# One core, agent attention and a mixture of experts: buffers of the experts' matrices, pacing of the token loads and the order of SyncE's queue

## The chip, the core and the metric

The kernel runs on one core of a Trainium2 chip. The core has five engines with queues of their own: TensorE (PE; PEld is its weight load), VectorE (DVE), ScalarE (ACT), GpSimd (POOL) and SyncE (SP), which computes nothing and issues most of the transfers. Sixteen DMA engines carry the transfers. The metric is the device time of one execution in microseconds (us), the median of the runs.

## What is computed

Four batches of 11456 tokens with 128 channels, 49 agents, 8 experts. Attention through agents gives one row for each token, and that row goes through one expert, a two-layer network whose hidden width is 1024:

```python
s = scale * agents @ k.T ; a2k = softmax(s over tokens) ; agent_v = a2k @ v
q2a = softmax(scale * q @ agents.T over agents) ; x = q2a @ agent_v
logits = normalise(x) @ normalise(expert_emb).T / tau
e = argmax(logits) ; gate = softmax(logits)[e]
out = gate * (relu(x @ w1[e]) @ w2[e])
```

Inputs and outputs are float32.

## The kernel before

**Units, tiles, steps.** The tokens of a batch are cut into 11 units of 128 x 8 tokens and one of 96 x 2. A unit of K, V or Q is one load of 512 KB (`unit_load`, L103 to L116) into the pool `ld`, 11 buffers that K, V, Q and also the two weight matrices of an expert (`load_expert`, L560 to L566) share. The expert layers run over tiles of 512 tokens, two to a unit: 23 tiles a batch, 8 hidden blocks f each, so 184 steps a batch and 736 in all. Step i is `ffn_mm1(i)` (L740, L741: two 512-column matmuls of high and low parts into hp; then hh on ACT, L744, and hl on DVE, L745) and `ffn_mm2(i - 4)` (L762 to L764: twelve 128-column matmuls into yp).

**One expert for a batch.** The kernel picks the likeliest expert of a batch (`pick_expert`, L487), reads its number on SP (`value_load`, L561: a TENSOR_LOAD), loads its w1 (w1s) and w2 (w2s), folds w1 with the batch's agent values into gh and gl (L520, L537, L538), splits w2 into w2h (ACT) and w2l (POOL, L550 and L551), and then the steps of that batch use gh, gl, w2h and w2l alone. Tokens of another expert ("strays") are marked and done one by one (`stray`).

**Work beside the steps.** While the steps of one batch run, generators do the rest, each advanced by a clock `now` of half steps; `yield n` puts a generator off by n steps. A K or Q unit: `split` squares and scales it on ACT (L313, L317), scales and subtracts it on POOL (L318, L319), and has SP transpose the result by DMA (L321, kT or qT); 8 steps later `scores` (L332 to L334, 24 small matmuls) stand behind the layers' last matmul on PE. A Q unit goes on to exponents (e) and a second transposing DMA (tt, L607), and after 8 more steps to its routing matmuls (rtp, L617 and L618); tt is what the layers' first matmul reads. A V unit: POOL subtracts (kd), ACT takes the exponent, PE multiplies (avp, L422).

**What sets the order.** The builder's scheduler orders every engine's instructions by a timeline of its own. Up to the first step SP is held to the order in which the code is traced (`manual_schedule`, L1082). From then on SP's order is the scheduler's as well, so loads and transposing DMAs stand on SP where its timeline puts them; `keys` (L1026) traces a load up to three units ahead of the K or V unit that is due, and `queries` (L1064) one Q unit ahead, all in one go. The due times of K and V are the table W_ (L1030), in parts of a batch's 184 steps.

Of the kernel before, what the change touches and what calls it, by code (L numbers as in the profile page):

```python
# [19 lines left out]
P = 128  # L20
# [10 lines left out]
def kernel(ctx: ExitStack, tc: tile.TileContext, q, k, v, agents, emb, tau, w1, w2, out):  # L31
# [24 lines left out]
    XB = 5  # L56

# [8 lines left out]
    ld = ctx.enter_context(tc.tile_pool(name="ld", bufs=11))  # L66
# [15 lines left out]

    def big(name, w=D):
        return ld.tile([P, UJ * W], F32, name=name, tag="ld")[:, : UJ * w].rearrange("p (c d) -> p c d", d=w)
# [4 lines left out]
    units = {}  # L89
# [13 lines left out]
    def unit_load(x, kind, b, u):  # L103
        if (kind, b, u) in units or b >= B or u >= NU:
            return
        p, n = ushape(u)
        one = kind == "v"
        s = big(kind + "t", W if one else D)
        if one:
            pool.memset(s[:, :, D:], 1.0)  # L110
        if u < NU - 1:
            src = x[b, : P * J, :].rearrange("(p j) d -> p j d", j=J)[:, u * UJ : u * UJ + n, :]
        else:
            src = x[b, P * J :, :].rearrange("(p j) d -> p j d", j=REM_J)
        sp.dma_start(out=s[:p, :n, :D], in_=src)
        units[kind, b, u] = s  # L116

# [183 lines left out]
    def split(kind, b, u, g):  # L301

        s = units[kind, b, u]
        p, n = ushape(u)

        while ffn_at[0] and len(xs_at) >= XB and not (xs_at[-XB] and now[0] >= xs_at[-XB] + 2 * XT):
            yield 1
        i = len(xs_at)
        xs_at.append(0)
        sq = sm.tile([P, 1], F32, name="usq", tag=kind + "usq", bufs=3)[:p]  # L310
        xs = wk.tile([P, UJ, 2, D], F16, name=kind + "s", tag="xs", bufs=XB)
        with in_place(h_last):
            act.activation(xs[:p, :n, 0], s[:p, :n], AF.Square, accum_out=sq)  # L313
        yield g
        hs = half_scale(sq, 14, kind + "u", 4, *([qbias] if kind == "q" else []))
        sc, iv = yield from hs
        act.activation(xs[:p, :n, 0], s[:p, :n], AF.Copy, scale=sc)  # L317
        pool.tensor_tensor(out=s[:p, :n], in0=s[:p, :n], in1=sc.unsqueeze(2).broadcast_to([p, n, D]), op=ALU.mult)  # L318
        pool.tensor_tensor(out=xs[:p, :n, 1], in0=s[:p, :n], in1=xs[:p, :n, 0], op=ALU.subtract)  # L319
        xT = wk.tile([P, 2 * UJ, P], F16, name=kind + "T", tag="xT", bufs=XB)  # L320
        sp.dma_start_transpose(out=xT[:, : 2 * n, :p], in_=xs[:p, :n].rearrange("p c h d -> p (c h d)"))  # L321
        xs_at[i] = now[0]
        return xT, iv
# [62 lines left out]
    def k1_f32(b, u):  # L386
# [5 lines left out]
        kT = pe_T(units["k", b, u], p, n)  # L392
        yield 2
# [10 lines left out]
    def k2_unit(b, u, eng, g):  # L404
# [15 lines left out]
        for c in range(n):  # L420
            hs = slice(LO * (c % 2), LO * (c % 2) + LO)
            pe.matmul(out=avp[hs, :W], lhsT=de[:p, c * A : c * A + LO], rhs=src[:p, c, :], start=(c < 2), stop=(c >= n - 2),  # L422
                      skip_group_check=True)
        if kb.k2 == 0:
# [135 lines left out]
    def load_expert(ei):  # L560
        ev = sp.value_load(ei[:1, :1], min_val=0, max_val=E - 1)  # L561
        w1s = big("w1s").rearrange("p a b -> p (a b)")
        w2s = big("w2s")
# [7 lines left out]
    def q_unit(b, u, g):  # L571
# [5 lines left out]
        if f32:  # L577
            xT = pe_T(units["q", b, u], p, n)
            yield 1
# [26 lines left out]
        else:  # L606
            sp.dma_start_transpose(out=tt[:, : n * p].rearrange("k (c p) -> k c p", p=p),  # L607
# [195 lines left out]
    def stray():  # L803
# [112 lines left out]
        yield 2  # L916
        h = big("sh")
        NH = 4
# [9 lines left out]
        for f in range(NF):  # L928
            pe.matmul(out=t_[:, :D], lhsT=h[:, f, :], rhs=w2s[:, f, :], start=(f == 0), stop=(f == NF - 1))
            if f % 2 == 1:  # L930
                yield 1
        o = sm.tile([P, D], F32, name="so", tag="so", bufs=1)
# [93 lines left out]
    def keys():  # L1026

        S = NT * NF

        W_ = [(0, 0.25, 0.3, 0.8), (-0.5, 0.25, 0.3, 0.8), (-0.5, 0.25, 0.3, 0.8)]  # L1030
        ops = []
        for b in range(1, B):
            k0, k1_, v0, v1 = (S * (b - 1 + x) for x in W_[b - 1])
            us = range(NEXT if b == 1 else 0, NU)
            ops += [(k0 + (k1_ - k0) * i / len(us), "k", b, u) for i, u in enumerate(us)]
            ops += [(v0 + (v1 - v0) * u / NU, "v", b, u) for u in range(NU)]
        ops.sort()
        start = now[0] // 2
        for i, (at, kind, b, u) in enumerate(ops):
            while now[0] // 2 < start + at:  # L1040
                yield 1
            for _, kd, lb, lu in ops[: i + 3]:
                unit_load(k if kd == "k" else v, kd, lb, lu)
# [20 lines left out]
    def queries():  # L1064
        for b in range(B):
            for u in range(NU):
                if b == 0 and u < LEAD:
                    continue
                for i in (b * NU + u, b * NU + u + 1):
                    unit_load(q, "q", i // NU, i % NU)  # L1070
                spawn(q_unit(b, u, (1, 8, 1, 1, 8, 2)), 2)
                yield UT * NF if u < NU - 1 else NF
# [14 lines left out]
    ffn_at[0] = now[0]  # L1087
    if B > 1:
# [3 lines left out]
    for i in range(nsteps):  # L1092
        b, t, f = ffn_steps[i]
        while not (hasattr(batches[b], "iall") and (b, unit_of(t)[0]) in tts):
            run_step()
        run_half()
        with tc.high_priority(200):
            ffn_mm1(i)
        if i >= LAG:
            step2(i - LAG)  # L1100
        run_half()
# [43 lines left out]
```

## Time and profile before

| | |
|---|---|
| time, median of 3 runs | 1070.23 us (1069.75 to 1071.07) |
| profiled execution, own time | 1072.67 us |
| its span (first to last instruction) | 1070.9 us |
| mean granted TensorE clock | 0.97 of 2.4 GHz |
| PE, PEld, DVE, ACT, POOL busy | 94%, 75%, 72%, 67%, 55% |
| moved by DMA | 152.63 MB, mean 143 GB/s |

The first step begins about 103 us into the span. The page gives shares of busy time over the whole span; the stretches differ, so the tables by stretch and the waits of single lines are read beside it. Matmuls are pipelined: a busy PE has work in flight, and the gaps before its instructions tell what it waited for.

### The profile page before, as it was taken

The page shows a single profiled execution, that of the slowest core. Times are in us where ns is not written, and L with a number is a line of the kernel's source. Part 1 is how long each engine was busy: PE and PEld are TensorE (multiplying, and loading weights), DVE is VectorE, ACT ScalarE, POOL GpSimd, SP SyncE. Part 2 cuts the span into 40 slices and gives each one's busy share as a digit, 9 for nine tenths or more (in the row PEclk, how much of TensorE's full clock was granted, in tenths as well). Part 3 has the DMA queues.
Part 4 walks back from the last instruction along what each step waited for, and adds up shares of the span by engine and source line. Part 5 has one row for each costly group of instructions (what it writes and reads, how often), then busy time and mean ns, then how long its engine had stood idle before and what let it go on. Part 6 is the DMA issues. An engine that isn't in the chain of part 4 may idle for free.

```text
span 1070.9 us, 33823 instructions
## 1 busy us (share of the span) xinstructions
PE 1008.5 (94%) x13878; PEld 806.6 (75%) x13878; DVE 769.5 (72%) x1779; ACT 722.6 (67%) x1406; POOL 583.8 (55%) x653
## 2 busy tenths in 40 slices
PE   7876989999997989999999898999999999999997
PEld 7764767777776877777777776777777777877776
DVE  5664777676687676676787776766678798677785
ACT  3445987676778776666777875766666666666553
POOL 2333995676667763746757774645444544543300
PEclk9776999999999999999999999999999999999999
DMA  9548999568649794557658997355136244442101
GB/s 337 162 103 224 233 227 243 120 148 193 113 113 269 158 202 121 120 138 179 150 95 231 215 190 143 83 129 133 45 72 176 59 127 91 104 80 61 47 31 36
DMA packets 283944, 152.63 MB, mean 143 GB/s; under 512 B 208315, under 2 KB 260619, under 8 KB 283787
## 3 DMA queue, kind: packets, MB, share of 16 engines
q1 hardware_dynamic: 270603, 126.98, 53.9%
q10 hardware_dynamic: 13120, 23.47, 6.4%
q8 instruction: 109, 1.79, 0.7%
q14 instruction: 48, 0.39, 0.1%
q0 software_dynamic: 64, 0.00, 0.0%
HBM read 75.80 MB, written 23.53 MB: 93 GB/s over the span
## 4 chain that ended last, share of the span: by engine, by line
PE 71%; DMA 10%; DVE 5%; POOL 5%; ACT 4%; issue 3%; SPq 0%; ACTq 0%; POOLq 0%; DVEq 0%
PE yp L762 12%; PE hp L740 12%; PE yp L764 11%; PE yp L763 11%; PE hp L741 11%; DMA kT<-ks 5%; PE avp L422 5%; DMA qT<-qs 2%; PE sp L396 2%; ACT hh L744 1%; PE sp L332 1%; DMA tt<-e 1%; PE fTp L378 1%; PE sp L333 1%; PE sp L334 1%
## 5 line engine op out<-in xcount | busy, mean ns | idle before, releaser
L745 DVE SCALAR_TENSOR_TENSOR hl<-hp,hh 128x512 f16<-128x512 f32 (+1 forms) x736 | 480.0, 670 | 167.5 <-ACT hh L744 147.7
L744 ACT ACTIVATE hh<-hp 128x512 f16<-128x512 f32 (+1 forms) x736 | 419.0, 591 | 225.1 <-PE yp L764 89.6
L762 PE MATMUL yp<-w2h,hh 128*128 128x128 f16 (+1 forms) x2880 | 519.2, 220 | 0.0
L763 PE MATMUL yp<-w2l,hh 128*128 128x128 f16 (+1 forms) x2880 | 518.8, 219 | 0.3 <-DVE w2l L548 0.3
L764 PE MATMUL yp<-w2h,hl 128*128 128x128 f16 (+1 forms) x2880 | 518.7, 219 | 0.0
L762 PEld LDWEIGHTS <-hh 128*128 128x128 f16 (+1 forms) x2880 | 284.6, 99 | 45.7 <-issue 6.1
L763 PEld LDWEIGHTS <-hh 128*128 128x128 f16 (+1 forms) x2880 | 284.3, 99 | 42.2 <-issue 0.6
L764 PEld LDWEIGHTS <-hl 128*128 128x128 f16 (+1 forms) x2880 | 284.0, 99 | 39.3 <-issue 0.5
L740 PE MATMUL hp<-tt,gh 128*128 128x512 f16 (+1 forms) x736 | 276.6, 376 | 3.0 <-DVE hl L745 3.0
L741 PE MATMUL hp<-tt,gl 128*128 128x512 f16 (+1 forms) x736 | 276.5, 376 | 0.0
L318 POOL TENSOR_TENSOR qt<-qt,hsc 128x1024 f32<-128x1024 f32 (+1 forms) x46 | 82.1, 1785 | 88.2 <-ACT qs L317 75.8
L319 POOL TENSOR_TENSOR qs<-qt,qs 128x1024 f16<-128x1024 f32 (+1 forms) x46 | 92.2, 2004 | 2.3
L599 POOL TENSOR_TENSOR e<-qe,e 128x392 f16<-128x392 f32 (+1 forms) x46 | 39.7, 862 | 98.2 <-ACT e L598 89.4
L740 PEld LDWEIGHTS <-gh 128*128 128x128 f16 x736 | 72.2, 98 | 7.5 <-issue 6.6
L741 PEld LDWEIGHTS <-gl 128*128 128x128 f16 x736 | 72.2, 98 | 5.9 <-issue 5.2
L318 POOL TENSOR_TENSOR kt<-kt,hsc 128x1024 f32<-128x1024 f32 (+1 forms) x36 | 64.3, 1786 | 22.3 <-ACT ks L317 22.0
L777 DVE TENSOR_TENSOR ot<-yp,gs 128x512 f32<-128x512 f32 (+1 forms) x92 | 61.8, 671 | 17.0 <-PE yp L764 16.3
L319 POOL TENSOR_TENSOR ks<-kt,ks 128x1024 f16<-128x1024 f32 (+1 forms) x36 | 72.7, 2021 | 0.9
L665 POOL TENSOR_TENSOR nrm<-quad,half 128x16 f32<-128x16 f32 (+2 forms) x28 | 68.2, 2435 | 2.0
L422 PE MATMUL avp<-vt,kd 128*64 128x129 f32 x720 | 60.6, 295 | 6.8 <-issue 3.9
L422 PEld LDWEIGHTS avp<-vt,kd 128*64 128x64 f32 x720 | 44.2, 144 | 23.2 <-issue 17.3
L634 POOL TENSOR_TENSOR rt<-rt,qe 128x392 f32<-128x392 f32 (+1 forms) x48 | 47.1, 981 | 26.5 <-ACT rt L633 25.6
(264 smaller groups left out, 1449.5 us busy)
## 6 DMA issues: line engine op xcount, KB each, us to landing
kt<-in_k_dram SPq DMA_DIRECT2D x44, 512.0 KB, 6.2
qt<-in_q_dram SPq DMA_DIRECT2D x44, 512.0 KB, 5.9
vt<-in_v_dram SPq DMA_DIRECT2D x44, 512.0 KB, 4.9
out_dram<-ot ACTq DMA_DIRECT2D x88, 256.0 KB, 2.1
w1s<-in_moe_w_dram SPq DMA_DIRECT2D x5, 512.0 KB, 3.7
w2s<-in_moe_w_dram SPq DMA_DIRECT2D x5, 512.0 KB, 5.3
qT<-qs SPq DMA_TRANSPOSE x46, 5.0
tt<-e SPq DMA_TRANSPOSE x46, 3.2
```

The costliest lines, as they stand in the source:

```text
L318: pool.tensor_tensor(out=s[:p, :n], in0=s[:p, :n], in1=sc.unsqueeze(2).broadcast_to([p, n, D]), op=ALU.mult)
L319: pool.tensor_tensor(out=xs[:p, :n, 1], in0=s[:p, :n], in1=xs[:p, :n, 0], op=ALU.subtract)
L422: pe.matmul(out=avp[hs, :W], lhsT=de[:p, c * A : c * A + LO], rhs=src[:p, c, :], start=(c < 2), stop=(c >= n - 2), skip_group_check=True)
L665: pool.tensor_tensor(out=nrm, in0=quad[:, :n], in1=half[:, :n], op=ALU.pow)
L740: pe.matmul(out=hp[:, :m], lhsT=bt.gh[:, fs], rhs=tt, start=True, stop=False)
L741: pe.matmul(out=hp[:, :m], lhsT=bt.gl[:, fs], rhs=tt, start=False, stop=True)
L744: h_last[:] = [act.activation(hh[:, :m], hp[:, :m], AF.Relu)]
L745: dve.scalar_tensor_tensor(out=hl[:, :m], in0=hp[:, :m], scalar=0.0, in1=hh[:, :m], op0=ALU.max, op1=ALU.subtract)
L762: pe.matmul(out=y, lhsT=hh[:, cs], rhs=bt.w2h[:, f, :], start=(f == 0 and c == 0), stop=False, skip_group_check=True)
L763: pe.matmul(out=y, lhsT=hh[:, cs], rhs=bt.w2l[:, f, :], start=False, stop=False, skip_group_check=True)
L764: y_last[:] = [pe.matmul(out=y, lhsT=hl[:, cs], rhs=bt.w2h[:, f, :], start=False, stop=last, skip_group_check=True)]
L777: dve.tensor_tensor(out=o[:p, :n], in0=yp[:p, :n], in1=gate, op=ALU.mult)
```

## The change

- w1s and w2s get a buffer each of their own (`bufs=1`); the pool `ld` shrinks from 11 buffers to 9 (LB).
- `used` and `room` keep a list of who took each `ld` buffer in turn and at which step its last reader was traced; a load in the layers is traced only when the buffer nine back was last read three steps ago or more.
- `plan` lists K, V and Q units with their due steps; a new generator, `loader`, traces at most one load a step, 18 steps ahead of the due step. `keys` and `queries` no longer load.
- In `split`, 5 steps lie between POOL's subtraction and the transposing DMA; before the DMA of tt, 4 steps. The 8 steps after each DMA stay.
- W_ of batch 1: K over 0 to 0.4 of a batch (was 0 to 0.25), V over 0.43 to 0.83 (was 0.3 to 0.8). Batches 2 and 3 keep theirs.
- The loop over the steps is traced under `manual_schedule` for SP: SP's order is that of the code there. The other engines stay the scheduler's.

```diff
-    ld = ctx.enter_context(tc.tile_pool(name="ld", bufs=11))
+    ld = ctx.enter_context(tc.tile_pool(name="ld", bufs=LB))          # LB = 9
+    ring = []
     def big(name, w=D):
+        ring.append([name, None])
+    def used(*unit):
+        ring[slot[unit]][1] = now[0]
+    def room():
+        at = ring[-LB][1] if len(ring) >= LB else -99
+        return at is not None and now[0] >= at + 2 * 3
 ...
         pool.tensor_tensor(out=xs[:p, :n, 1], in0=s[:p, :n], in1=xs[:p, :n, 0], op=ALU.subtract)
+        used(kind, b, u)
+        if ffn_at[0]:
+            yield 5
         xT = wk.tile([P, 2 * UJ, P], F16, name=kind + "T", tag="xT", bufs=XB)
         sp.dma_start_transpose(out=xT[:, : 2 * n, :p], in_=xs[:p, :n].rearrange("p c h d -> p (c h d)"))
 ...
-        w1s = big("w1s").rearrange("p a b -> p (a b)")
-        w2s = big("w2s")
+        w1s = ld.tile([P, F], F32, name="w1s", tag="w1s", bufs=1)
+        w2s = ld.tile([P, NF, D], F32, name="w2s", tag="w2s", bufs=1)
 ...
         else:
+            if ffn_at[0]:
+                yield 4
             sp.dma_start_transpose(out=tt[:, : n * p].rearrange("k (c p) -> k c p", p=p),
 ...
-        W_ = [(0, 0.25, 0.3, 0.8), (-0.5, 0.25, 0.3, 0.8), (-0.5, 0.25, 0.3, 0.8)]
+        W_ = [(0, 0.4, 0.43, 0.83), (-0.5, 0.25, 0.3, 0.8), (-0.5, 0.25, 0.3, 0.8)]
+    AHEAD2 = 18
+    def loader():
+        kv, qs = plan()
+        start = now[0] // 2
+        X = {"k": k, "v": v, "q": q}
+        for at, kind, b, u in sorted(kv + qs):
+            if (kind, b, u) in units:
+                continue
+            while now[0] // 2 < start + at - AHEAD2 or not room():
+                yield 1
+            unit_load(X[kind], kind, b, u)
+            yield 1
 ...
-            for _, kd, lb, lu in ops[: i + 3]:
-                unit_load(k if kd == "k" else v, kd, lb, lu)
 ...
-                for i in (b * NU + u, b * NU + u + 1):
-                    unit_load(q, "q", i // NU, i % NU)
-                spawn(q_unit(b, u, (1, 8, 1, 1, 8, 2)), 2)
-                yield UT * NF if u < NU - 1 else NF
+            while now[0] // 2 < start + at + 2:
+                yield 1
+            spawn(q_unit(b, u, (1, 8, 1, 1, 8, 2)))
 ...
-    for i in range(nsteps):
+    spawn(loader())
+    with tc.manual_schedule(engines={mybir.EngineType.SP}):
+        for i in range(nsteps):
 ...
```

What the two built programs then hold, at three places. The names are the tiles with their numbers; DMA lines are loads, DMA_TRANSPOSE lines the transposing DMAs.

SP, near the end of batch 0's steps, behind the second batch's expert read and weight loads. Before:

```order
L321 DMA_TRANSPOSE kT_5846<-ks_5732 128x16x128
L607 DMA_TRANSPOSE tt_5778<-e16_1_152 128x8x128
L321 DMA_TRANSPOSE qT_5977<-qs_5870 128x16x128
L115 DMA kt_6091<-in_k_dram 128x1024
L115 DMA qt_6314<-in_q_dram 128x1024
L115 DMA kt_6450<-in_k_dram 128x1024
L115 DMA kt_6739<-in_k_dram 128x1024
L115 DMA qt_6741<-in_q_dram 128x1024
L115 DMA kt_7057<-in_k_dram 96x256
L115 DMA qt_7186<-in_q_dram 128x1024
L321 DMA_TRANSPOSE kT_6197<-ks_6125 128x16x128
```

The same place on SP now:

```order
L338 DMA_TRANSPOSE kT_5939<-ks_5599 128x16x128
L629 DMA_TRANSPOSE tt_5851<-e16_1_152 128x8x128
L338 DMA_TRANSPOSE qT_6057<-qs_5766 128x16x128
L128 DMA kt_6176<-in_k_dram 128x1024
L128 DMA qt_6228<-in_q_dram 128x1024
L338 DMA_TRANSPOSE kT_6296<-ks_6032 128x16x128
L629 DMA_TRANSPOSE tt_6398<-e16_0_151 128x8x128
L128 DMA kt_6562<-in_k_dram 128x1024
L338 DMA_TRANSPOSE qT_6564<-qs_6350 128x16x128
L338 DMA_TRANSPOSE kT_6621<-ks_6428 128x16x128
```

Seven loads stood in a row ahead of a transposing DMA; now there are two, then one, between transposing DMAs.

SP, just before the first step, around the first batch's expert read. Before:

```order
L321 DMA_TRANSPOSE qT_748<-qs_721 128x16x128
L607 DMA_TRANSPOSE tt_816<-e16_0_151 128x8x128
L321 DMA_TRANSPOSE kT_836<-ks_804 128x16x128
L321 DMA_TRANSPOSE kT_1109<-ks_855 128x16x128
L561 TENSOR_LOAD e0i_877
```

The same place on SP now:

```order
L338 DMA_TRANSPOSE qT_748<-qs_721 128x16x128
L128 DMA kt_1062<-in_k_dram 128x1024
L128 DMA qt_1105<-in_q_dram 128x1024
L128 DMA kt_1121<-in_k_dram 128x1024
L128 DMA kt_1166<-in_k_dram 128x1024
L128 DMA qt_1195<-in_q_dram 128x1024
L629 DMA_TRANSPOSE tt_816<-e16_0_151 128x8x128
L338 DMA_TRANSPOSE kT_836<-ks_804 128x16x128
L580 TENSOR_LOAD e0i_877
```

Five loads of the layers' stage came ahead of the expert read, and one transposing DMA went behind it.

POOL, where the second batch's w2 is split (w2s, then w2l). Before:

```order
L318 TENSOR_TENSOR kt_5372<-kt_5372,hsc_6148 128x1024
L669 TENSOR_TENSOR nrm_5879<-ls_5882,nrm_5879 128x8
L550 TENSOR_TENSOR w2s_5610<-w2s_5610,hsc_6049 128x1024
L453 MEMSET avT_16054 128x128
L319 TENSOR_TENSOR ks_6125<-kt_5372,ks_6125 128x8x128
L676 TENSOR_TENSOR lga_5872<-lga_5872,cc_5919 128x64
L551 TENSOR_TENSOR w2l_5833<-w2s_5610,w2h_5832 128x1024
```

The same place on POOL now:

```order
L332 TENSOR_TENSOR qt_5592<-qt_5592,hsc_6373 128x1024
L698 TENSOR_TENSOR lga_6017<-lga_6017,cc_6066 128x64
L333 TENSOR_TENSOR qs_6350<-qt_5592,qs_6350 128x8x128
L707 TENSOR_SCALAR el_6120<-esa_6018 128x8
L708 TENSOR_TENSOR el_6120<-el_6120,l_6026 128x8
L569 TENSOR_TENSOR w2s_5825<-w2s_5825,hsc_6206 128x1024
L472 MEMSET avT_16025 128x128
L332 TENSOR_TENSOR kt_5787<-kt_5787,hsc_6449 128x1024
L570 TENSOR_TENSOR w2l_5987<-w2s_5825,w2h_5986 128x1024
```

A Q unit's two large operations moved ahead of the split of w2 and a K unit's subtraction behind it.

Two counts along the whole orders, of hh on ACT and of hp on PE. From a unit's scaled copy on ACT (L317) to its first score matmul on PE (L332) there lie, over the units in the layers, 10 to 19 steps before (mean 15 for K, 13 for Q) and 15 to 31 now (mean 19 for K, 20 for Q). And the second batch's gp matmuls (L520), which need its w1s, stand at step 165 before and at step 177 now; that batch's steps begin at 184.

## Rows read from the trace of the kernel before

**Rows 1.** The page: PE over the span, and its slices.
```profile
PE 1008.5 (94%) x13878; PEld 806.6 (75%) x13878; DVE 769.5 (72%) x1779; ACT 722.6 (67%) x1406; POOL 583.8 (55%) x653
...
L740 PE MATMUL hp<-tt,gh 128*128 128x512 f16 (+1 forms) x736 | 276.6, 376 | 3.0 <-DVE hl L745 3.0
```

**Rows 2.** Stretches of 25 us: busy of each engine, granted clock, DMA share, GB/s.
```profile
core 0: us, PE busy (x) PEld busy (x) DVE busy (x) ACT busy (x) POOL busy (x), PEclk, DMA share, GB/s
...
125.00:150.00 25.00, 23.06 (x365) 18.20 (x362) 18.25 (x47) 22.54 (x44) 24.67 (x23) 1.00 1.10 187
150.00:175.00 25.00, 22.87 (x372) 18.61 (x373) 17.52 (x40) 20.67 (x38) 21.81 (x19) 1.00 1.16 254
...
325.00:350.00 25.00, 19.34 (x280) 15.09 (x279) 17.03 (x42) 18.87 (x37) 20.20 (x22) 0.90 1.09 266
...
425.00:450.00 25.00, 25.00 (x342) 19.52 (x341) 18.96 (x37) 18.59 (x36) 18.38 (x20) 1.00 0.47 117
...
1025.00:1050.00 25.00, 25.00 (x315) 19.42 (x313) 18.58 (x44) 13.68 (x23) 0.09 (x1) 1.00 0.09 33
```

**Rows 3.** PE's waits, whole span: for what, us in total, times, longest us.
```profile
engine line waited for: us in total, times, longest us
PE sp L332 <- DMA kT<-ks: 18.2, 8, 5.7
...
PE rtp L617 <- DMA tt<-e: 3.7, 3, 1.8
...
PE sp L332 <- DMA qT<-qs: 3.0, 4, 1.8
PE hp L740 <- DVE hl L745: 3.0, 3, 2.2
```

**Rows 4.** The longest such wait: ACT's copy, then the chain of work.
```profile
327.26 1.16 ACT L317 ACTIVATE ks<-kt,hsc 128x1024 f16<-128x1024 f32 x1
...
332.89 2.09 POOL ks L319
335.01 12.93 DMA kT<-ks
347.94 0.05 issue
347.99 0.22 PE sp L332
```

**Rows 5.** SP's DMAs of L321: how long SP stood, ns, and landing.
```profile
L321 SPq DMA_TRANSPOSE qT<-qs x46: 1180/2364/7407, 61.3 to 992.3; - x46
L321 SPq DMA_TRANSPOSE kT<-ks x36: 1181/2938/7696, 84.6 to 662.7; - x36
...
DMA to landing us min/median/max: 2.3/5.1/12.9
```

**Rows 6.** Short stretches from the three longest waits on, columns as in Rows 2.
```profile
342.00:348.00 6.00, 0.34 (x3) 0.02 (x2) 2.14 (x5) 3.00 (x5) 5.79 (x4) 0.76 1.14 184
348.00:352.00 4.00, 4.00 (x52) 3.98 (x53) 0.98 (x2) 0.92 (x2) 0.57 (x2) 0.51 1.20 281
...
403.00:406.00 3.00, 3.00 (x32) 1.87 (x31) 0.75 (x2) 2.41 (x5) 1.49 (x2) 0.52 0.01 3
...
652.00:655.00 3.00, 3.00 (x33) 1.81 (x31) 0.75 (x2) 2.42 (x5) 1.43 (x2) 0.55 0.03 6
```

**Rows 7.** Start-up: ACT's wait for a K unit, PE's first step.
```profile
70.67 1.06 ACT L313 ACTIVATE ks<-kt 128x1024 f16<-128x1024 f32 x1 [2.89 <-DMA kt<-in_k_dram]
...
102.77 0.61 PE L740 MATMUL hp<-tt,gh 128*128 128x512 f16 x1
```

**Rows 8.** The chain that ended last, in order of time: start us, us, what.
```profile
91.72 6.88 DMA w2s<-in_moe_w_dram
98.62 1.15 ACT w2h L541 x2
```

**Rows 9.** The split of the second batch's w2 on POOL.
```profile
335.19 2.15 POOL L551 TENSOR_TENSOR w2l<-w2s,w2h 128x1024 f16<-128x1024 f32 x1
```

**Rows 10.** SP's own waits from 104 us on: total us, times, longest us.
```profile
SPq L115 <- PE avp L422: 96.1, 17, 10.7
```

More of the change, by code (lines that the diff above doesn't have):

```diff
@@ L56 @@
     XB = 5
+    LB = 9
     groups = [[0]]
@@ L88 @@
     now = [0]
-    units = {}
+    units, slot = {}, {}
+    def used(*unit):
[3 more added lines that the diff above has]
+        return at is not None and now[0] >= at + 2 * 3
     def tshape(t):
@@ L116, in unit_load @@
         units[kind, b, u] = s
+        slot[kind, b, u] = len(ring) - 1
     a_sb = sm.tile([A, B, C], F32, name="a_sb", tag="a_sb", bufs=1)
@@ L392, in k1_f32 @@
         kT = pe_T(units["k", b, u], p, n)
+        used("k", b, u)
         yield 2
@@ L423, in k2_unit @@
                       skip_group_check=True)
+        used("v", b, u)
         if kb.k2 == 0:
@@ L578, in q_unit @@
             xT = pe_T(units["q", b, u], p, n)
+            used("q", b, u)
             yield 1
@@ L916, in stray @@
         yield 2
+        while not room():
+            yield 1
         h = big("sh")
+        hs = len(ring) - 1
         NH = 4
@@ L931, in stray @@
                 yield 1
+        ring[hs][1] = now[0]
         o = sm.tile([P, D], F32, name="so", tag="so", bufs=1)
@@ L1024, in first, with plan @@
             now_run(batches[0].pick)
-    def keys():
-        S = NT * NF
-        W_ = [(0, 0.25, 0.3, 0.8), (-0.5, 0.25, 0.3, 0.8), (-0.5, 0.25, 0.3, 0.8)]
-        ops = []
+    S = NT * NF
+    def plan():
+        W_ = [(0, 0.4, 0.43, 0.83), (-0.5, 0.25, 0.3, 0.8), (-0.5, 0.25, 0.3, 0.8)]
+        kv, qs, at = [], [], 0
         for b in range(1, B):
@@ L1034, in keys @@
             us = range(NEXT if b == 1 else 0, NU)
-            ops += [(k0 + (k1_ - k0) * i / len(us), "k", b, u) for i, u in enumerate(us)]
-            ops += [(v0 + (v1 - v0) * u / NU, "v", b, u) for u in range(NU)]
-        ops.sort()
-        start = now[0] // 2
-        for i, (at, kind, b, u) in enumerate(ops):
+            kv += [(k0 + (k1_ - k0) * i / len(us), "k", b, u) for i, u in enumerate(us)]
+            kv += [(v0 + (v1 - v0) * u / NU, "v", b, u) for u in range(NU)]
+        for b in range(B):
+            for u in range(NU):
+                if b > 0 or u >= LEAD:
+                    qs.append((at, "q", b, u))
+                    at += UT * NF if u < NU - 1 else NF
+        return sorted(kv), qs
+    AHEAD2 = 18
+    def loader():
+        kv, qs = plan()
+        start = now[0] // 2
+        X = {"k": k, "v": v, "q": q}
[6 more added lines that the diff above has]
+            yield 1
+    def keys():
+        start = now[0] // 2
+        for at, kind, b, u in plan()[0]:
             while now[0] // 2 < start + at:
                 yield 1
-            for _, kd, lb, lu in ops[: i + 3]:
-                unit_load(k if kd == "k" else v, kd, lb, lu)
             if kind == "k":
@@ L1064, in queries @@
     def queries():
[L1065 to L1068, printed above, removed]
-                for i in (b * NU + u, b * NU + u + 1):
-                    unit_load(q, "q", i // NU, i % NU)
-                spawn(q_unit(b, u, (1, 8, 1, 1, 8, 2)), 2)
-                yield UT * NF if u < NU - 1 else NF
+        start = now[0] // 2
+        for at, _, b, u in plan()[1]:
+            while now[0] // 2 < start + at + 2:
+                yield 1
+            spawn(q_unit(b, u, (1, 8, 1, 1, 8, 2)))
     def step2(i):
@@ L1091 @@
     spawn(stray_first(), (B - 1) * NT * NF + 8)
-    for i in range(nsteps):
[L1093 to L1101, printed above, removed]
+    with tc.manual_schedule(engines={mybir.EngineType.SP}):
+        for i in range(nsteps):
+            b, t, f = ffn_steps[i]
+            while not (hasattr(batches[b], "iall") and (b, unit_of(t)[0]) in tts):
+                run_step()
+            run_half()
+            with tc.high_priority(200):
+                ffn_mm1(i)
+            if i >= LAG:
+                step2(i - LAG)
+            run_half()
     for i in range(nsteps - LAG, nsteps):
```

## The prediction

> **What bounds the kernel now.** I read the page first: PE is busy 94% of the span, the other engines 55 to 75% [rows 1]. Busy says little about pipelined matmuls, so I went on to the table by stretch. In most stretches PE is busy for all 25.00 us at clock 1.00, as in the pair that stands for them here [rows 2]: there PE sets the pace and no change of the loads can help. PE is short in other stretches, 19.34 of 25 us from 325 on and about 23 from 125 to 175, and in just these the DMA share is 1.09 to 1.16, against 0.47 and less in the full ones [rows 2]. PE's waits name the cause: 18.2 us for kT, 3.0 for qT and 3.7 for tt [rows 3], all outputs of transposing DMAs that SP issues. That is 24.9 us in 15 waits, and each holds up the layers' matmuls queued behind the scores, since PE works in order.
>
> The longest shows how such a wait comes about. ACT's scaled copy of a K unit starts at 327.26, POOL ends its part at 334.98, SP begins the transposing DMA at 335.01, and it lands 12.93 us later [rows 4]; the median is 5.1 and the least 2.3 [rows 5]. SP itself stands 7.7 us at the slowest, 2.9 in the median [rows 5]. Seven loads stand in a row ahead of that DMA in SP's order. So the delay is a burst: the loads are traced in bunches and go to the DMA engines all at once, and the transposing DMA comes after them.
>
> **The change, part by part.** The sum is made against the profiled execution's own time, 1072.67 us (its span is 1070.9), and carried over to the median by 1070.23 / 1072.67 = 0.9977.
>
> A step lasts (1070.9 - 102.8 - about 5 of tail) / 736 = 1.31 us, from the first hp [rows 7] and the count of L740 [rows 1].
>
> *Waits for transposing DMAs.* Two parts act on them. First, the distance from ACT's copy to the scores grows from 10 to 19 steps (mean 14) to 15 to 31 (mean 19.7): by 5.5 steps or 7.2 us, and at the least 15 steps are 19.6 us. The longest chain of the trace took 347.94 - 327.26 = 20.7 us [rows 4]; that unit stood at 12 steps and its successors at the same place of the second batch stand at 26 or more. Every wait of PE for kT was 5.7 us or less [rows 3], so 7.2 us covers each even if no DMA gets faster. Second, with at most two loads in a row the landing should fall back from 12.9 towards the median. W_ of batch 1 adds to this: ten K units over 74 steps rather than 46, in the stretches with share 1.10 and 1.16 [rows 2]. Bounds: 0 to -24.9. I take nine tenths, -22.4, since the cover exceeds the longest wait; the tenth is for waits that SP's fixed order brings back.
>
> *The clock.* After each of the three longest waits the granted clock is 0.51, 0.52 and 0.55, that is 1.2 rather than 2.4 GHz, for 4, 3 and 3 us [rows 6]; PE had been idle just before. Lost: 4 x 0.49 + 3 x 0.48 + 3 x 0.45 = 4.8 us. If the waits go, so does this. Bounds 0 to -4.8; I take -4.
>
> *Start-up.* Up to the first step the pool of 9 makes each load wait for the reader of the buffer nine back instead of eleven. The first K units hide that, since their loads run far ahead of PE. The one place that shows is the first K unit of batch 1: its buffer now comes from the first V unit, so ACT, which works in order, may wait for it as it waited 2.9 us for the second such unit [rows 7]. On the other side w1s and w2s wait for no buffer, one transposing DMA less stands ahead of the expert read (SP stands 2.9 us at a median one), and w2s, whose 6.88 us DMA ends the chain just before ACT squares it [rows 8], comes earlier. -5 to +5; I take -1.
>
> *The experts' chain of batch 1.* Its gp matmuls now stand 7 steps (9.2 us) ahead of the batch's first step instead of 19. What follows them: ACT's copies, DVE's, and POOL's split, which ended at 335.19 + 2.15 = 337.3 [rows 9], about 14 steps ahead of the first step and 18 ahead of the first yp. Twelve steps later it still has 6 steps, or 8 us. A Q unit's two POOL operations of 2 us each now stand ahead of it; they fit. I put 0 to +5 on it.
>
> *SP in program order.* An entry that waits holds those behind it, and these are the transposing DMAs PE waits for. DMAs of kT and qT come 5 steps after POOL's work and those of tt 4, so SP should find their data ready; `room` traces a load only 3 steps after its buffer's last reader. 0 to +5 for the waits that remain. With the experts' chain together I take +3 of 0 to +10.
>
> *No cost:* the list kept by `used` and `room` is bookkeeping at build time, with no instruction. The number of matmuls, copies and DMAs is unchanged, so what PE does in its full stretches stays.
>
> Sum: 1072.67 - 22.4 - 4 - 1 + 3 = 1048.3; times 0.9977 it is **1046 us**.
>
> **The rivals.**
>
> *The DMA engines themselves are the bound.* Share 1.10 and 1.16 over 50 us, and again 1.09 from 325 [rows 2], could mean that the engines have no time left, and then no order on SP makes a transposing DMA land sooner: the bytes are the same. PE's waits would stay, later in the order, and little but the clock and start-up terms moves: 1072.67 - 6 = 1066.7, or about 1064, and if the clock stays low, 1068: 1066. Against it: the share is 0.47 or less elsewhere [rows 2], so there is room to spread into, and the added distance alone covers the longest wait. [...] Chance 0.08.
>
> *Head of the queue.* SP waits in order for POOL. If POOL runs more than 5 steps (6.5 us) behind the code in the dense stretches, as its 24.67 busy of 25 us from 125 on would allow [rows 2], half of the waits and of the lost clock return: 1072.67 - 11.2 - 2 - 1 + 3 = 1061.5, or 1059. Against: K of batch 1 is spread over 1.6 times the steps, so POOL has room there. Chance 0.14.
>
> *Slower: loads that wait for a buffer.* In the layers SP stood at loads until avp matmuls freed a buffer: 96.1 us in 17 waits, the longest 10.7 [rows 10]. There are now 9 buffers, and transposing DMAs can't pass such a load. If the wait reaches 10.7, it exceeds the added 7.2 us of distance by 3.5, and PE loses that. It turns the result once 24.4 / 3.5 = 7 of the 17 are so long; with 9 it is 1046 + 9 x 3.5 = 1078. Against: `room`, and two buffers no longer held by experts' matrices. Chance 0.08.
>
> **How the numbers follow.** The forecast, 1036 to 1056, has 0.65; below it (every wait gone, start-up better by 5) 0.04; half the gain 0.14; DMA engines, spread around 1066, 0.08; slower 0.08, and 0.01 more for what no row shows. The range 1035 to 1066 leaves out half of the DMA engines' case, the slower one and most of what lies below, and so holds about 0.84. A measurement of this kernel can tell some 0.2% from no change, that is 1068.1 to 1072.4. Faster by more: 0.65 + 0.04 + 0.14 + half of the DMA engines' case, 0.04, is 0.87; the other half is the same, 0.04; slower 0.09.
>
> **What would show it.** In the profile after: PE's waits for kT, qT and tt fall from 24.9 us to under 5; the stretches from 325 to 425 and from 575 to 675 show clock 1.00 and PE above 24 of 25; the longest landing of L338 (L321 before) falls from 12.9 to under 9, and SP's longest stand from 7.7 to under 5. The first step starts within 5 us of 102.8. If the DMA engines are the bound, the waits stand at the same shares; if SP's head is, SP's waits for POOL in front of the transposing DMAs stand beside PE's; if buffers are, its waits for avp grow above 96. It is wrong if PE's waits vanish and the time doesn't follow, which would mean that PE's idle time wasn't what set the end, or if waits for hh, hl or w2l take their place.

## The result

The changed kernel takes 1057.51 us (median of 4 runs, 1052.91 to 1059.72), beside 1070.65 us for the kernel before in the same comparison. The ratio is 0.9861 with an interval of 0.9829 to 0.9894: 13 us faster by the medians and 15 by the ratio, where 24 were forecast. The profiled execution took 1056.05 us, with a span of 1054.2, against 1072.67 and 1070.9.

In the changed kernel's line numbers L327 to L333 are `split`, L338 is the transposing DMA of kT and qT (L321 before), L349 the scores, L629 the DMA of tt (L607), L639 its readers, L128 a load (L115), L580 the expert read, L762 the first layer and L767 hl.

The page's busy line (for [rows 1]), then what PE waited for over the span (us in total, times, longest us), the counterpart of [rows 3]:

```profile
PE 1002.8 (95%) x13878; PEld 802.2 (76%) x13878; DVE 771.4 (73%) x1779; ACT 729.4 (69%) x1406; POOL 581.6 (55%) x653
```

```profile
PE sp L349 <- DMA kT<-ks: 7.2, 5, 3.5
...
PE hp L762 <- DVE hl L767: 6.4, 7, 3.5
...
PE rtp L639 <- DMA tt<-e: 2.6, 3, 1.7
...
PE sp L349 <- DMA qT<-qs: 2.2, 3, 0.9
```

The waits for transposing DMAs fell from 24.9 to 12.0 us, by 12.9. Those for hl rose from 3.0 to 6.4. Where the remaining waits lie, the stretches of 25 us show (busy us of PE, PEld, DVE, ACT and POOL, granted clock, DMA share, GB/s), the counterpart of [rows 2]; the last row is six us long and stands behind the longest wait left for a transposing DMA, 3.5 us at 586:

```profile
150.00:175.00 25.00, 25.00 (x390) 20.04 (x388) 19.55 (x45) 22.42 (x41) 21.96 (x20) 1.00 1.05 191
...
350.00:375.00 25.00, 22.46 (x338) 17.20 (x336) 18.18 (x38) 19.36 (x37) 19.86 (x18) 1.00 0.81 188
375.00:400.00 25.00, 23.52 (x375) 18.92 (x374) 18.62 (x38) 16.74 (x34) 14.10 (x18) 1.00 0.88 185
...
575.00:600.00 25.00, 20.81 (x303) 16.99 (x300) 15.34 (x38) 17.10 (x36) 16.81 (x11) 0.86 0.97 199
```

```profile
590.00:596.00 6.00, 6.00 (x54) 4.34 (x54) 2.09 (x5) 3.32 (x5) 5.30 (x3) 0.51 0.94 195
```

From 125 to 175 PE is full now, even at a share of 1.05. It is still short around the starts of the second and third batch, whose steps begin at 339.1 and 583.0 us. SP's DMAs of L338 (ns that SP stood, min/median/max, then us to landing) land no sooner in the median (5.8 us, 5.1 before) and lost little of their tail, against [rows 5]:

```profile
L338 SPq DMA_TRANSPOSE qT<-qs x46: 1185/2232/4811, 64.5 to 981.2; - x46
L338 SPq DMA_TRANSPOSE kT<-ks x36: 1552/3281/6239, 82.5 to 649.0; - x36
...
DMA to landing us min/median/max: 2.4/5.8/11.4
```

What has changed is what SP itself waits for. From 104 us on (as [rows 10]), first the kernel before, then the changed one:

```profile
SPq L607 <- POOL e L599: 151.4, 25, 12.3
```

```profile
SPq L629 <- POOL e L619: 170.8, 19, 19.3
...
SPq L580 <- DVE e L525: 38.0, 2, 22.4
...
SPq L128 <- PE avp L440: 15.3, 7, 3.5
```

SP's waits at loads for avp fell from 96.1 us to 15.3. In their place SP stands longer at the DMAs of tt, 423.8 us in 43 waits when all reasons are added up (207.3 in 40 before), and at the expert read (55.9, before 31.0). A wait of SP costs nothing unless something behind it is ready. Here something is. First SP, then POOL, then PE, from 332 us on (start us, us, operation; idle before and its releaser in brackets):

```profile
332.77 5.36 SPq L338 DMA_TRANSPOSE kT<-ks  x1
349.97 1.23 SPq L629 DMA_TRANSPOSE tt<-e  x1
351.30 0.52 SPq L128 DMA_DIRECT2D kt<-in_k_dram  x1
351.92 3.38 SPq L338 DMA_TRANSPOSE qT<-qs  x1
355.39 2.74 SPq L338 DMA_TRANSPOSE kT<-ks  x1
```

```profile
330.01 2.13 POOL L333 TENSOR_TENSOR qs<-qt,qs 128x1024 f16<-128x1024 f32 x1
...
339.67 2.14 POOL L333 TENSOR_TENSOR ks<-kt,ks 128x1024 f16<-128x1024 f32 x1
...
349.04 0.91 POOL L619 TENSOR_TENSOR e<-qe,e 128x392 f16<-128x392 f32 x1
```

```profile
357.76 0.20 PE L349 MATMUL sp<-a,qT 128*128 128x49 f16 x1 [0.89 <-DMA qT<-qs]
```

SP is free at 338.1 and next in its order is tt, whose e POOL ends at 349.95: a stand of 11.8 us. Behind it, the qs that POOL ended at 332.1 goes out at 351.9 and the ks that it ended at 341.8 at 355.4, 19.8 and 13.6 us later. PE then waits for qT (0.9 us) and for kT (1.1 us) in turn. The same happens at 565 to 576 and at 599 to 611, with waits of PE behind each: the longest that is left, 3.5 us, is for a ks that was ready at 562.2 and went out at 581.3. Behind a shorter stand, 586 to 590, PE waits for nothing. Over all steps, with POOL's subtractions and SP's DMAs of kT and qT paired in their order, these DMAs go out at most 7.8 us after POOL in the kernel before and 42 us in all; in the changed kernel it is up to 22.5 us, and 477 us in all.

### The profile page after: what moved, and what is told of

It reads as the page before. It is cut to its first block, busy times and chain, and to the rows that moved or that the text cites. A ratio compares the mean times of both kernels' runs of the same rounds, so it can differ in the third digit from the quotient of the medians.

```text
span 1054.2 us, 33839 instructions
## 1 busy us (share of the span) xinstructions
PE 1002.8 (95%) x13878; PEld 802.2 (76%) x13878; DVE 771.4 (73%) x1779; ACT 729.4 (69%) x1406; POOL 581.6 (55%) x653
## 4 chain that ended last, share of the span: by engine, by line
PE 84%; DMA 6%; DVE 5%; issue 2%; ACT 1%; POOL 1%; SPq 0%; POOLq 0%; ACTq 0%
PE yp L784 14%; PE yp L786 14%; PE yp L785 14%; PE hp L762 14%; PE hp L763 13%; PE avp L440 4%; DMA kT<-ks 2%; PE sp L414 2%; PE sp L349 1%; PE sp L350 1%; DMA qT<-qs 1%; PE sp L351 1%; PE fTp L395 1%; DMA w1s<-in_moe_w_dram 1%; DVE hl L767 1%
## 5 line engine op out<-in xcount | busy, mean ns | idle before, releaser
L767 DVE SCALAR_TENSOR_TENSOR hl<-hp,hh 128x512 f16<-128x512 f32 (+1 forms) x736 | 482.6, 671 | 163.8 <-ACT hh L766 141.3
L762 PE MATMUL hp<-tt,gh 128*128 128x512 f16 (+1 forms) x736 | 275.2, 374 | 6.5 <-DVE hl L767 6.4
L332 POOL TENSOR_TENSOR qt<-qt,hsc 128x1024 f32<-128x1024 f32 (+1 forms) x46 | 82.0, 1783 | 51.0 <-ACT qs L331 48.1
L333 POOL TENSOR_TENSOR qs<-qt,qs 128x1024 f16<-128x1024 f32 (+1 forms) x46 | 92.3, 2007 | 1.6
L332 POOL TENSOR_TENSOR kt<-kt,hsc 128x1024 f32<-128x1024 f32 (+1 forms) x36 | 64.3, 1787 | 42.2 <-ACT ks L331 39.9
L762 PEld LDWEIGHTS <-gh 128*128 128x128 f16 x736 | 72.0, 98 | 6.8 <-issue 5.6
L333 POOL TENSOR_TENSOR ks<-kt,ks 128x1024 f16<-128x1024 f32 (+1 forms) x36 | 72.6, 2017 | 0.8
L689 POOL TENSOR_SCALAR l<-rtg 128x16 f32<-128x16 f32 (+2 forms) x28 | 7.3, 262 | 90.6 <-ACT rtg L654 88.8
```

What stands on the lines that cost most here:

```text
L762: pe.matmul(out=hp[:, :m], lhsT=bt.gh[:, fs], rhs=tt, start=True, stop=False)
L767: dve.scalar_tensor_tensor(out=hl[:, :m], in0=hp[:, :m], scalar=0.0, in1=hh[:, :m], op0=ALU.max, op1=ALU.subtract)
```

## The experiments

Two questions: which part of the change brought the gain (distance, pacing of the loads, buffers, spread), and what kept the other half. Each run is compared with the kernel before on its own chip. "In the steps" means from the first hp of the profiled execution to its last; waits over the whole span can hold some that stand ahead of the first step. Runs 1 to 4 share a chip, and so do 5 to 8 and 9 to 11.

**1. The distance alone, on the kernel before**

```diff
+        if ffn_at[0]:
+            yield 5
         xT = wk.tile([P, 2 * UJ, P], F16, name=kind + "T", tag="xT", bufs=XB)
...
+            if ffn_at[0]:
+                yield 4
             sp.dma_start_transpose(out=tt[:, : n * p].rearrange("k (c p) -> k c p", p=p),
```

> The kernel before, with the 5 steps ahead of the transposing DMA of kT/qT and the 4 ahead of that of tt, and nothing else: loads still come in rows of up to 8, SP's order in the layers is the scheduler's. From ACT's copy to the scores there lie 14 to 31 steps (mean 19). If distance is what took PE's waits away: PE's waits for kT, qT and tt fall from 24.9 us to 12 or less, and the time is about 1070.5 - 12 - 2 for the clock = 1056. If it was the pacing of the loads: the waits stay above 18 us and the time is 1066 or more.

Measured: 1066.95 us (1061.98 to 1069.69) against 1072.99, ratio 0.9946 (0.9924 to 0.9968). PE's waits in this run (L334 is the scores, L621 the readers of tt), then SP at the place of [rows 4] (here L323 is the DMA of kT and qT, L611 that of tt):

```profile
PE rtp L621 <- DMA tt<-e: 8.5, 5, 3.7
...
PE sp L334 <- DMA kT<-ks: 5.6, 3, 2.4
```

```profile
332.43 0.34 SPq L115 DMA_DIRECT2D kt<-in_k_dram  x1
333.75 8.15 SPq L323 DMA_TRANSPOSE kT<-ks  x1
342.00 1.24 SPq L611 DMA_TRANSPOSE tt<-e  x1
```

The waits for kT did fall, from 18.2 to 5.6 us, but those for tt rose from 3.7 to 8.5: behind eight loads SP stands 8.15 us at a transposing DMA (7.7 at the most before), and now tt, next in the queue, is what comes late: PE waits 3.7 us for it until 347.8. The waits, 14.1 us, lie between the two theories; the time is the one that the pacing theory expected. The distance is worth 6 us, less than half of the gain, and 1.8 of that stand ahead of the first step (101.0 us).

**2. The changed kernel without the distance**

```diff
-        if ffn_at[0]:
-            yield 5
...
-            if ffn_at[0]:
-                yield 4
```

> The changed kernel without those 5 and 4 steps: loads paced, SP in program order, 10 to 22 steps from ACT's copy to the scores (mean 14), as before. If distance did it: PE's waits for kT, qT and tt are back above 20 us, time 1066 to 1072, and more if SP, now meeting its DMAs before POOL is done, holds up others. If pacing did it: waits of 12 us or less, time within 3 us of the changed kernel's 1057.5.

Measured: 1057.61 us (1057.1 to 1065.75), ratio 0.9883 (0.9831 to 0.9936), with 17.9 us of waits for the three tiles, none longer than 1.9. The time is that of the changed kernel, as the pacing theory has it, though its waits are not the 12 us or less that it expected: there are more of them, and short. The first step came at 95.7 us, 2.3 earlier than in the changed kernel, and the steps took 950.9 us against 947.5. So the distance may be worth some 3 us in the steps; one profiled execution of each can't show that.

**3. SP's order in the layers left to the scheduler**

```diff
-    with tc.manual_schedule(engines={mybir.EngineType.SP}):
+    with nullcontext():
         for i in range(nsteps):
```

> The changed kernel, but with SP's order over the layers left to the scheduler instead of the program's. In the changed kernel SP stood 22 us at the second batch's expert read and 10 to 12 us at single DMAs of tt, with kT's DMAs that had their data behind them. If that order costs the remaining 12 us of PE's waits: waits of 5 us or less, time 1047 to 1051. If the DMA engines, or POOL's lateness, cost it: waits of 10 us or more, time within 3 us of 1057.5.

Measured: 1052.24 us (1050.08 to 1055.25), ratio 0.9818 (0.978 to 0.9855), under every run of experiment 2 on that chip and of the changed kernel in experiment 5. PE's waits:

```profile
PE rtp L639 <- DMA tt<-e: 8.8, 5, 3.2
...
PE sp L349 <- DMA kT<-ks: 0.8, 1, 0.8
```

Time and waits (9.6 us over the span) lie between the two expectations. Without the program's order the waits for kT fall from 7.2 to 0.8 us and none for qT remain; tt is what is left. In the steps the waits for the three tiles are 5.7 us, all for tt, against 11.7 in the changed kernel. SP's waits at tt, from 104 us on, are 77.3 us instead of 423.8. The first step comes at 101.0 us, 3 later than in program order, so the steps themselves gain some 9: 938.6 us from the first hp to the last, against 947.5. Of these 9 us, 6.0 are the waits for the three tiles and 2.5 those for hl (6.4 to 3.9), while those for gh rise by 2.1.

**4. The buffers alone, on the kernel before**

```diff
-    ld = ctx.enter_context(tc.tile_pool(name="ld", bufs=11))
+    ld = ctx.enter_context(tc.tile_pool(name="ld", bufs=9))
...
-        w1s = big("w1s").rearrange("p a b -> p (a b)")
-        w2s = big("w2s")
+        w1s = ld.tile([P, F], F32, name="w1s", tag="w1s", bufs=1)
+        w2s = ld.tile([P, NF, D], F32, name="w2s", tag="w2s", bufs=1)
```

> The kernel before, with w1s and w2s in buffers of their own and 9 buffers in the pool, and nothing else. The smaller pool alone breaks up the rows of loads: at most 3 stand in a row in the layers instead of 7, and the distances stay at 9 to 19 steps (mean 14). If bursts of loads were the cause of PE's waits: waits fall from 24.9 us to under 15 and the time to 1058 or less. If distance is what counts: waits stay above 20 us, time 1064 to 1071, of which the start-up gives back up to 5 us (first step at 98 instead of 102.8).

Measured: 1063.85 us (1061.33 to 1065.41), ratio 0.9904 (0.9874 to 0.9934), with 20.7 us of waits for the three tiles and the first step at 101.1. The waits are those that were expected if distance counts, and the time is just below that range; neither is what was expected if bursts were the whole cause. The smaller pool is worth 9 us, of which 1.7 are the start-up, with rows of at most three loads on SP in the layers. The waits add up to little less, but the longest is 3.6 us rather than 5.7.

**5. The changed kernel once more**

> The changed kernel itself once more, so that the next runs have it beside them on their chip: within 4 us of 1057.5, PE's waits for kT, qT and tt near 12 us.

Measured: 1057.18 us (1056.82 to 1058.29), ratio 0.9852 (0.9819 to 0.9885); waits of 12.8 us. This is what 6 to 8 stand beside.

**6. Scheduler's order and no distance** (the edits of 2 and 3 together)

> The changed kernel with SP's order over the layers left to the scheduler, and without the 5 and 4 steps: loads paced, 10 to 21 steps from copy to scores (mean 14). With the steps, this order gave 1052.2 and waits of 8.8 us. If distance is worth something once loads are paced: waits of 15 us or more and 1057 to 1062. If pacing alone carries the gain: waits near 9 us and 1052, as with them.

Measured: 1053.8 us (1051.27 to 1059.58), ratio 0.9829 (0.9778 to 0.9881), waits of 15.5 us. With the distance it was 1052.24: the runs don't tell them apart. The waits came as the distance theory expected, the time as the other did. In the steps the waits are 11.7 us here and 5.7 in experiment 3, and the steps took 941.4 and 938.6 us.

**7. tt's DMA five steps later in SP's order**

```diff
             if ffn_at[0]:
-                yield 4
+                yield 9
```

> The changed kernel, 9 steps instead of 4 between POOL's e and the transposing DMA of tt; all else as it is, SP in program order. If the wait at tt (SP stood 10 to 12 us at three of them, with kT's DMAs whose data were ready behind) is what leaves PE's waits for kT: those waits fall from 7.2 us to under 3 and the time to 1051 to 1054. If the expert read or the DMA engines are: no change, 1056 to 1060.

Measured: 1052.35 us (1051.29 to 1054.58), ratio 0.981 (0.9774 to 0.9845), under every run of experiment 5 on the same chip. The waits, and two stretches of it:

```profile
PE sp L349 <- DMA kT<-ks: 5.1, 4, 1.5
PE sp L349 <- DMA qT<-qs: 1.5, 2, 1.0
...
PE rtp L639 <- DMA tt<-e: 0.4, 1, 0.4
```

```profile
125.00:150.00 25.00, 25.00 (x397) 20.26 (x396) 19.56 (x44) 22.62 (x42) 20.15 (x16) 1.00 1.14 221
...
175.00:200.00 25.00, 25.00 (x383) 20.03 (x382) 19.23 (x41) 18.90 (x37) 13.41 (x20) 1.00 1.16 252
```

SP's waits at tt fell from 426.8 us to 63.8, PE's waits for the three tiles from 12.8 to 7.0 and the time by 4.8, as expected of SP's stand at tt, although kT kept 5.1 us and not under 3. All bytes are the same, and tt goes out later, not earlier. The two stretches speak on the rival of the DMA engines: at a share of 1.14 and 1.16 PE loses nothing.

**8. The old due times of the second batch**

```diff
-        W_ = [(0, 0.4, 0.43, 0.83), (-0.5, 0.25, 0.3, 0.8), (-0.5, 0.25, 0.3, 0.8)]
+        W_ = [(0, 0.25, 0.3, 0.8), (-0.5, 0.25, 0.3, 0.8), (-0.5, 0.25, 0.3, 0.8)]
```

> The changed kernel with the old due times of the second batch: K over 0 to 0.25 of a batch, V over 0.3 to 0.8. If spreading these K units is a part of the gain: DMA share above 1.0 from 100 to 175 us, PE's waits of 3 to 6 us come back there, and the time is 1061 to 1064. If paced loads alone do it: within 3 us of the changed kernel beside it.

Measured: 1062.48 us (1059.78 to 1064.42), ratio 0.9904 (0.987 to 0.9938): 5 us slower than experiment 5, so the spread is a part of the gain. Its mechanism is not settled. From 125 to 150 us the DMA share is 1.09 and PE is 1.6 us short of full, with 1.2 us of waits for qT and kT between 142 and 150, not the 3 to 6 that were expected; over the span the waits are 13.2 us, as many as without this edit, and the profiled execution is 3 us longer, of which 0.7 are start-up and 1.6 waits for gh at batch starts (2.4 against 0.8).

**9. Loads in fours**

```diff
-        for at, kind, b, u in sorted(kv + qs):
-            if (kind, b, u) in units:
-                continue
+        todo = [o for o in sorted(kv + qs) if o[1:] not in units]
+        for j, (_, kind, b, u) in enumerate(todo):
+            at = todo[j - j % 4][0]
             while now[0] // 2 < start + at - AHEAD2 or not room():
                 yield 1
             unit_load(X[kind], kind, b, u)
-            yield 1
```

> The changed kernel, with the loader tracing four loads in one go (all four due with the first of them) instead of one a step; buffers, distances, due times and SP in program order stay. If it is the pacing of loads that gives the gain: transposing DMAs land late behind the fours again, PE's waits for kT, qT and tt rise from 12 us to 18 or more and the time to 1062 to 1067. If the smaller pool and the spread K units suffice: within 3 us of 1057.2.

Measured: 1072.98 us (1064.46 to 1073.69), ratio 0.9997 (0.9972 to 1.0023). The whole gain is gone, more than expected, with buffers, distance, spread and program order in place. One of its longest waits, on SP and then on PE:

```profile
154.05 0.57 SPq L128 DMA_DIRECT2D kt<-in_k_dram  x1
154.67 0.43 SPq L128 DMA_DIRECT2D qt<-in_q_dram  x1
155.15 0.43 SPq L128 DMA_DIRECT2D kt<-in_k_dram  x1
155.62 0.42 SPq L128 DMA_DIRECT2D vt<-in_v_dram  x1
156.16 8.33 SPq L338 DMA_TRANSPOSE qT<-qs  x1
164.66 4.89 SPq L338 DMA_TRANSPOSE kT<-ks  x2
```

```profile
167.40 0.22 PE L349 MATMUL sp<-a,qT 128*128 128x49 f16 x1 [4.14 <-DMA qT<-qs]
```

And the stretch around it, columns as above:

```profile
150.00:175.00 25.00, 20.86 (x302) 16.74 (x299) 15.07 (x34) 16.71 (x32) 16.73 (x14) 0.86 0.80 163
```

Four loads go out in 2 us; the transposing DMA behind them holds SP for 8.33 us and lands after 11.2, and the next one waits for SP. (Its qs had been ready since 149.0: SP had stood at tt until 152.8, as it does in the changed kernel too.) Waits for the three tiles are 25.5 us, 21.8 of them in the steps, nearly as before the change (24.9). The share over 150 to 175 is 0.80 here, less than in the changed kernel (1.05) in whose same stretch PE was full. Three of the lost us are the start-up (first step at 100.8), where eight loads instead of five go out ahead of the expert read. The run shows that the gain needs paced loads under this order on SP; it doesn't show that pacing alone makes it, since the buffers alone gave 9 us (experiment 4) and the spread 5 (experiment 8).

**10. Program order for 40 steps, then the scheduler's**

```diff
-    with tc.manual_schedule(engines={mybir.EngineType.SP}):
-        for i in range(nsteps):
+    def run_steps(lo, hi):
+        for i in range(lo, hi):
...
+    with tc.manual_schedule(engines={mybir.EngineType.SP}):
+        run_steps(0, 40)
+    run_steps(40, nsteps)
```

> The changed kernel, with SP in program order for the first 40 steps and from there in the scheduler's. The start-up of program order (first step at 97.8 us, scheduler's order 101.0) and the steps of the scheduler's order (938.7 us from the first hp to the last, program order 947.6) should then add up: 97.8 + 938.7 + 8.6 of tail = 1045 span, 1047 time. If the start-up's 3 us are given back in the steps (the loads that were held up come later): 1050 to 1053.

Measured: 1052.77 us (1050.82 to 1058.37), ratio 0.9855 (0.9821 to 0.9888). This is the second expectation: the start-up gain did not come over whole (first step at 100.0, though five loads go out ahead of the expert read as in the changed kernel), and 7.2 us of waits for tt stayed.

**11. The same, with tt's readers later**

```diff
-            spawn(q_unit(b, u, (1, 8, 1, 1, 8, 2)))
+            spawn(q_unit(b, u, (1, 8, 1, 1, 12, 2)))
```

> As the run before it (program order for 40 steps, then the scheduler's), with 12 steps instead of 8 between the transposing DMA of tt and the matmuls that read it. Under the scheduler's order all of PE's waits for transposing DMAs were 8.8 us for tt. If that distance is what they lack: they fall under 2 us and the time by 5 to 7 us, to 1041 to 1044. If tt's DMA then only moves later or something else is late (hl, gh): within 2 us of the run before it.

Measured: 1044.58 us (1042.73 to 1047.52), ratio 0.9768 (0.974 to 0.9795). Its interval lies below those of the changed kernel (0.9819 to 0.9885 in experiment 5) and of experiment 10 on the same chip. Its median is the lowest of all the kernels run, 26.5 us ahead of the kernel before; the intervals of experiments 3, 6 and 7 reach into its own.

```profile
PE rtp L639 <- DMA tt<-e: 1.7, 3, 0.9
...
PE sp L349 <- DMA qT<-qs: 1.1, 2, 0.6
...
PE sp L349 <- DMA kT<-ks: 0.6, 1, 0.6
```

All waits for transposing DMAs together are 3.4 us, not the 2 that were expected, and the time fell by 8.2 us rather than 5 to 7. Of the 7.4 us between the two profiled executions, 1.9 are the start-up (first step at 98.1).

**12. The same four steps in program order throughout** (only the diff of 11, on the changed kernel)

> The changed kernel, SP in program order throughout, with 12 steps instead of 8 between the transposing DMA of tt and the matmuls that read it, nothing else. In the changed kernel SP stands at tt's DMAs and delays kT's behind them; this edit moves only the readers of tt, not the order on SP around it. If SP's stand is what costs, kT's waits stay (near 7 to 10 us) and the time is 1054 to 1058, tt's own waits of 1 to 3 us aside. If the longer distance of tt alone gave the last run its 8 us: 1047 to 1050 here too.

Measured: 1055.12 us (1051.83 to 1057.8), ratio 0.986 (0.9794 to 0.9926), with 7.7 us of waits for kT and 4.5 for qT. In program order the longer distance of tt gives nothing that can be measured; SP's stand at tt remains (429.2 us of waits there, 65.9 in experiment 11), and what is behind it comes late.

The table puts the medians together:

| loads, SP's order | with the 5 and 4 steps | without |
|---|---|---|
| as before, scheduler's | 1066.95 | 1072.99 |
| paced, program's | 1057.18 | 1057.61 |
| paced, scheduler's | 1052.24 | 1053.8 |
| in fours, program's | 1072.98 | not run |

## Why the prediction was right and wrong

The range held the time and the sign was right. The point did not: 1046 was forecast, and 1057.5 lies above the 1036 to 1056 that were given 0.65. The time is that of the rival named head of the queue, 1059, to which 0.14 was given. That the range held is owed to this rival's place in it, not to the sum. By the steps of the sum, on the profiled executions:

- *Waits for transposing DMAs:* taken at -22.4, measured -12.9. This is the step that failed, in two ways. First, "7.2 us covers each even if no DMA gets faster" set the distance against one wait at a time. Experiment 1 did just that and left 14.1 us: a burst does not delay one DMA but all that stand behind it, and covering kT made tt the next in line. Second, "the tenth is for waits that SP's fixed order brings back" was too small. Of the 11.7 us left in the steps, 6.0 go when the order is left to the scheduler (experiment 3). The rest are waits for tt, and four more steps ahead of its readers take a part of those (6.5 us in experiment 10, 1.4 in experiment 11). The pacing, named second and without a price of its own, is what the gain can't do without (experiment 9), while the distance is worth 6 us with bursts and nothing that these runs can measure without them. "At most two loads in a row" held only at the place shown: in the trace twelve rows of three or four loads go out in the steps, eight of them within 1.7 to 3.1 us. They lie where PE waits for no transposing DMA, from 199 to 218, 401 to 495 and 650 to 736 us.
- *The clock:* taken at -4. By the same working one such stretch is left, 6 us at 0.51, the level of 1.2 GHz, behind a wait of PE: 2.9 us lost rather than 4.8, so -1.9. The working left out a fourth stretch of the kernel before, from its first step on, at 0.50; from 98 to 101 us, at its own first step, the changed kernel has 1.00. That is another -1.7, and -3.6 in all: near the -4, but not by the stretches that were counted.

```profile
102.77:106.20 3.43, 3.43 (x15) 1.19 (x12) 2.38 (x8) 3.43 (x8) 2.65 (x3) 0.50 1.13 292
```

- *Start-up:* taken at -1 of -5 to +5, measured -4.8 (first step at 98.00 us, [rows 7]). The feared wait came, ACT stood 2.83 us for the first K unit of batch 1, but only took the place of the 2.9 us for the second. The transfer of w2s, 6.88 us in [rows 8], was no longer in the chain; that of w1s was, shorter, and issued 2.35 us earlier than in the kernel before (88.75 against 91.10). The runs with eight loads ahead of the expert read start 3 us later (experiments 3, 4 and 9); no run varied that number alone. So the size was off, within the bounds given.

```profile
65.08 1.06 ACT L327 ACTIVATE ks<-kt 128x1024 f16<-128x1024 f32 x1 [2.83 <-DMA kt<-in_k_dram]
```

```profile
88.75 3.97 DMA w1s<-in_moe_w_dram
```

```profile
98.00 0.38 PE L762 MATMUL hp<-tt,gh 128*128 128x512 f16 x1
```

- *Experts' chain and SP's order:* taken at +3. The experts' chain cost next to nothing: PE waited 1.0 us in all for gh (1.5 before) and 1.0 for w2l (0.3). SP's order is priced by experiments 3 and 5 at some 5 us of the whole, about 9 in the steps less 3 at the start, and most of it is in the waits above. The waits, the clock and the start-up come to -12.9 - 3.6 - 4.8 = -21.3, and -16.6 was measured. Of the 4.7 us between, 3.4 are a term that the sum didn't have: the waits for hl rose by that much, and those for hh and w2l by 1.2. All of PE's idle time in the steps fell from 30.0 to 20.8 us.

Of the rivals, *head of the queue* named the right mechanism at the wrong entry. It feared that kT's DMA would meet POOL's subtraction unfinished; in fact SP stood at tt for POOL's e, with kT's data ready behind (experiments 3 and 7). *The DMA engines* are ruled out as a bound that their mean share would show: PE is full at 1.16 in experiment 7 and loses 4.14 us at a share of 0.80 in experiment 9. The prediction's own reading, that PE is short in just the stretches with shares of 1.09 to 1.16 and full at 0.47 or less, came from the rows picked. The same table of the kernel before has these:

```profile
400.00:425.00 25.00, 22.44 (x307) 17.56 (x308) 15.89 (x33) 15.42 (x33) 8.56 (x10) 0.93 0.48 122
...
475.00:500.00 25.00, 25.00 (x373) 19.70 (x370) 17.56 (x40) 19.81 (x40) 19.01 (x22) 1.00 0.85 202
```

The order of SP's entries is what counts: in experiment 9 the same bytes in another order cost 15.8 us against experiment 5. The Trainium skill ("DMA: Bandwidth & Descriptors", section "Issuing engines are not separate DMA queues") says that starting DMAs on several engines at once saves only the sequencer's time for the start, usually small beside the DMA itself. For a transposing DMA behind loads it is not small here: SP stood 8.33 us at one that landed after 11.2. No run here moved the transposing DMAs to a second engine. *Loads that wait for a buffer* did not come: SP's waits for avp fell to 15.3 us.

Of the signs named in advance, the first step came within 5 us of 102.8, and the longest landing (12.9 to 11.4 us) and SP's longest stand at an issue (7.7 to 6.2) moved the right way, but not under 9 and 5. The waits under 5 us and full stretches from 325 to 425 and from 575 to 675 did not come. SP's waits for POOL beside PE's were the sign named for head of the queue, and that is what the trace has. Of the signs of being wrong, one came in part: waits for hh, hl and w2l rose from 3.3 to 7.9 us.

## What to carry to other kernels

A queue that issues both bulk loads and transfers someone waits for should be fed the loads one at a time where the waits are: in experiment 9 SP stood 8 us at the transposing DMA behind four loads, and the distance, still in place, did not cover all that stood behind it. The changed kernel's own rows of four, in stretches without such waits, cost PE nothing. When such a queue is put in program order, every entry that may meet unfinished data belongs behind those whose data are ready; look in the trace for a stand of the queue with finished producers behind it. A distance is priced by the whole queue behind the late entry, not by the one wait it was measured on.

## What the runs showed of the hardware

The largest wait for hl in the changed kernel, 3.5 us from 857 us on, is one that none of the edits above was aimed at. The kernel before has one like it, 2.2 us at 883, so it makes 1.3 us of the rise of 3.4. DVE, then POOL there, in the changed kernel:

```profile
856.60 3.02 DVE L896 SCALAR_TENSOR_TENSOR aTs<-aT_all,msk,aTs 128x49 f32<-128x49 f32 x1
...
862.53 0.25 DVE L896 SCALAR_TENSOR_TENSOR aTs<-aT_all,msk,aTs 128x49 f32<-128x49 f32 x1
```

```profile
856.07 1.31 POOL L852 DMA_INDIRECT xq<-in_q_dram,ix  x1 [0.19 <-DVE eq L873]
857.42 2.13 POOL L333 TENSOR_TENSOR qs<-qt,qs 128x1024 f16<-128x1024 f32 x1
```

The same small operation takes 0.25 us a little later; here it ends at 859.62, with POOL's subtraction (859.55), and hl stands behind it on DVE. The Trainium skill says on this that DVE with two inputs from SBUF and GpSimd take a shared pair of ports in turn, for a whole instruction ("SBUF — State Buffer", section "SBUF: two separate sides"). The rows agree with that, and so do the traces of the other kernels. Over all 14 traces the operations that write aTs run 56 times. In 34 of them no operation of POOL was under way at their start, and they took 0.23 to 0.31 us. The other 22 took 0.24 to 3.02 us, and each ended within 0.2 us of the end of an operation on POOL. No run was made to vary this alone.
